# Order and due times of the transposing transfers of q and k in a chunked-attention and gated-FFN kernel

## The chip, the core and the metric

One core of one Trainium2 chip runs the whole program. The metric is the device time of one execution in microseconds (us), the median of several runs. The engines are named as in the profile: PE (TensorE, matmuls), PEld (its weight loads), DVE (VectorE), ACT (ScalarE), POOL (GpSimd, which here issues the loads from memory through the queue that the profile calls q0, software_dynamic) and SP (SyncE, which here issues the stores and the transposing transfers through q1, hardware_dynamic).

## What is computed

Attention over chunks of 32 rows, each with 8 memory keys, 16 rows of left and 8 rows of right context, then a gated feed-forward network over all 3072 rows (4 batches of 768), cut from the reference:

```python
for c in range(nc):                       # S // 32 = 24 chunks for each of 4 x 8 heads
    k_full = np.concatenate([mem_k, k[:, :, l_start:r_end]], axis=2)
    v_full = np.concatenate([mem_v, v[:, :, l_start:r_end]], axis=2)
    scores = scale * np.matmul(q_c, k_full.transpose(0, 1, 3, 2))
    scores = scores - np.max(scores, axis=-1, keepdims=True)
    a = np.exp(scores)
    a = a / (np.sum(a, axis=-1, keepdims=True) + 1e-09)
    out[:, :, c_start:c_end] = np.matmul(a, v_full)
...
gate = np.maximum(x @ w_gate, 0.0)        # x: 3072 x 512, w_gate and w_val: 512 x 1536
return ((gate * (x @ w_val)) @ w_out)     # w_out: 1536 x 512
```

## The kernel before

The 3072 rows are 24 tiles of 128 rows, numbered a = 0 to 23, six to a batch. Each tile goes through one chain of steps. q and k of the tile are loaded by POOL (`load_qk`, line 187). Both are transposed, so that the head's 64 elements lie on the partitions. `scores` (line 234) is 32 small matmuls on PE; row maximum, subtraction, row sum, reciprocal and normalisation are on DVE and the exponent on ACT. The probabilities p are transposed, `values` (line 305) multiplies them with v on PE, and `x_copy` brings the result to the block's x tile. The feed-forward network runs over seven blocks of 3, 3, 4, 4, 4, 4 and 2 tiles. A block is 12 pairs of groups of four matmuls, gate and value (`first`, line 325, the tiles g_ps and v_ps, from a ring of four PSUM buffers named fps), each pair with a relu on ACT and a product on DVE, and then, for each of its tiles, four groups of three matmuls that give out_ps (`second`, line 351). A copy on ACT to o_sb and a store by SP (`store`, line 359) end each tile. The attention of later tiles is woven between the matmuls of the network.

The transposition is done in two ways. For tiles below LATE_QK = 15, PE transposes q and k into PSUM (`qk_t`) and ACT or DVE copies them out (`qk_copy`). From tile 15 on, SP issues a transposing transfer from SBUF to SBUF (`qk_transfer`, line 214). That of q (called q15, q16 and so on below) lands in its place in qT. That of k (k15, k16, ...) lands in k_t, a ring of three buffers, and a key copy on ACT or DVE (`qk_copy`, lines 78 and 80 in the profile) spreads it into kT between the memory keys. The probabilities of tiles from LATE_P = 18 on are transposed by SP too (`p_transfer`, line 297). `scores` of tile a needs q of a and the key copies of a and, inside a batch, of a + 1; tile 17 is the last of its batch.

No engine chooses at run time. `schedule()` (line 568) simulates the kernel with costs written by hand and writes down one fixed instruction order for each engine; on the chip each engine goes through its order and waits on semaphores for what an instruction needs. An instruction that waits holds up all that stands behind it on its engine. The costs that touch the transposing transfers stand on one line:

```python
ISSUE, LAND, SLACK, LAND_P = 1.4, 12.0, 8.0, 3.0    # line 418
```

ISSUE is the time that SP is taken to be busy with one transfer. LAND is the time after which q may be used and the key copy may be planned. SLACK is how long after the planned landing of the load the transfer may be planned. LAND_P is the landing time of the transfer of p. These numbers only place instructions in the orders; the semaphores keep the result right whatever they are. The ring sizes (`room`, line 372) hold 3 k_t, 4 fps, 3 o_sb and 2 PSUM tiles for attention (aps).

Of the kernel before, what the change touches and what calls it, by code (L numbers as in the profile page):

```python
# [20 lines left out]
def kernel(  # L21
# [12 lines left out]
    nc = tc.nc  # L34
# [262 lines left out]
    def p_transfer(a):  # L297
        PT[a] = smpool.tile([128, HP, 128], F16, name="pT", bufs=6)
        nc.sync.dma_start(PT[a], P_n.pop(a).rearrange("p h a s -> p (h a s)"), transpose=True)
# [75 lines left out]
    def op(key, eng, fn, deps=(), prio=(0,), take=(), give=(), after=()):  # L375
        ops[key] = dict(eng=eng, fn=fn, deps=list(deps), prio=prio, take=list(take), give=list(give),
                        after=list(after))
# [4 lines left out]
    def psum(n):  # L382
        return {"ACT": 0.21 + 0.83e-3 * n, "DVE": 0.22 + 1.04e-3 * n}

    engine = {"ACT": nc.scalar, "DVE": nc.vector}
    MARGIN = 0.4


# [26 lines left out]
        return [("f", blk - 1, m, 0)] if m >= 0 else [("f", blk - 2, m + NDC, 0)]  # L415


    ISSUE, LAND, SLACK, LAND_P = 1.4, 12.0, 8.0, 3.0

    def pace_t(a):  # L420
        return [("s", a - 4)]
# [1 line left out]
    for a in range(NT):  # L423
        b, t = divmod(a, TPB)
        last = t == TPB - 1
        for i in (1, 0):
            if a >= LATE_QK:
                op(("t", a, i), {"SP": ISSUE}, lambda e, a=a, i=i: qk_transfer(a, i),
                   [(("qk", a, i), SLACK), ("new", b)],
                   (1, a - i, 0), ["kt"] if i else [], [("qk", LAND)], pace_t(a))  # L430
                if i:
                    op(("tc", a, i), {"DVE": 0.4, "ACT": 0.6}, lambda e, a=a, i=i: qk_copy(a, i, engine[e]),
                       [(("t", a, i), LAND)], (1, a - i, 0), (), ["kt"])
                continue
            op(("t", a, i), {"PE": 0.24}, lambda e, a=a, i=i: qk_t(a, i), [("qk", a, i), "ib", ("new", b)],
               (1, a - i, 0), ["aps"], ["qk"], pace(max(a - i, 0)))
            op(("tc", a, i), psum(HP * 128), lambda e, a=a, i=i: qk_copy(a, i, engine[e]), [("t", a, i)],
               (1, a - i, 0), (), ["aps"])
        op(("s", a), {"PE": 0.36}, lambda e, a=a: scores(a),
           [(("t", a, 0), LAND) if a >= LATE_QK else ("tc", a, 0), ("tc", a, 1)] + ([] if last else [("tc", a + 1, 1)]), (1, a, 1), ["sps"],  # L440
           ["kv"] if last else [], [("s", a - 1)] if a else [])
        op(("max", a), {"DVE": 0.74 + (0.2 if t == 0 or last else 0)}, lambda e, a=a: row_max(a), [("s", a)],
           (1, a, 2), ["mx"])
        op(("sub", a), {"DVE": 0.74}, lambda e, a=a: subtract(a), [("max", a)],
           (1, a, 3), ["dif"], ["sps", "mx"])
        op(("exp", a), {"ACT": 1.15}, lambda e, a=a: exponent(a), [("sub", a)], (1, a, 4), ["p"], ["dif"])
        op(("sum", a), {"DVE": 0.74}, lambda e, a=a: row_sum(a), [("exp", a)], (1, a, 5), ["sm"])
        op(("rec", a), {"DVE": 0.24}, lambda e, a=a: reciprocal(a), [("sum", a)], (1, a, 6), ["rinv"], ["sm"])
        op(("nrm", a), {"DVE": 0.74}, lambda e, a=a: normalise(a), [("rec", a)], (1, a, 7), ["pn"], ["p", "rinv"])
        if a < LATE_P:  # L450
            op(("p", a), {"PE": 0.24}, lambda e, a=a: p_t(a), [("nrm", a)], (1, a, 8), ["aps"], ["pn"])
            op(("pc", a), psum(HP * 128), lambda e, a=a: p_copy(a, engine[e]), [("p", a)], (1, a, 9), ["pT"], ["aps"])
        else:
            op(("pc", a), {"SP": ISSUE}, lambda e, a=a: p_transfer(a), [("nrm", a)], (0, a), ["pT"], [("pn", LAND_P)])
        blk = block_of[a]
        j = a - starts[blk]
        op(("v", a), {"PE": 0.45}, lambda e, a=a: values(a),
           [("pc", a) if a < LATE_P else (("pc", a), LAND_P)] + [("vl", b, 0 if b else t // 3, n) for n in range(2 if b else 2 * HP)]
           + ([("mr", b, n) for n in range(2 * HP)] if b else []), (1, a, 10), ["aps"] + (["xT"] if j == 0 else []), ["pT"],
           [("v", a - 1)] if a else [])  # L460
        op(("x", a), psum(HP * 128), lambda e, a=a: x_copy(a, engine[e]), [("v", a)], (1, a, 11), (), ["aps"],
           [("x", a - 1)] if a else [])
# [105 lines left out]
    def schedule():  # L568
# [20 lines left out]
        def ready(o, t, margin=0.0):  # L589
            if any(d not in started for d in o["after"]):  # L590
                return False
            for d in o["deps"]:
                d, lag = d if timed(d) else (d, 0.0)
                if d not in done or done[d] + lag + margin > t + 1e-9:
                    return False
            return all(room[r] >= o["take"].count(r) for r in o["take"])

        while len(started) < len(ops) + len(loads):
            t = heapq.heappop(times)
            while times and times[0] <= t + 1e-9:  # L600
                heapq.heappop(times)
            for g in [g for g in gives if g[0] <= t + 1e-9]:
                gives.remove(g)
                room[g[1]] += 1
            flying = [f for f in flying if f > t]
            moved = True
            while moved:
                moved = False
                for e in ("POOL", "PE", "ACT", "DVE", "SP"):
                    if free[e] > t + 1e-9:  # L610
                        continue
                    if e == "POOL":
                        if n_load == len(loads):
                            continue
                        o = loads[n_load]
                        if len(flying) >= 8 or not ready(o, t):
                            continue
                        n_load += 1
                        key = o["key"]
                        if o["n"]:  # L620
                            end = t + 0.62 + 0.27e-3 * o["n"]
                            queue_end = max(queue_end, end + 0.8) + o["work"]
                            flying.append(queue_end + 1.0)
                            done[key] = queue_end + (1.2 if n_load < 8 else 2.4 if n_load < 45 else 6.0 if key[0] == "vl" else 4.0)
                        else:
                            end = done[key] = t + max(o["work"], 0.6)
                        fn = o["fn"]
                    else:
                        o = None
                        for _, key in todo[e]:  # L630
                            late_pe = e == "PE" and t > 36.0 and ops[key]["prio"][0] == 1
                            if ready(ops[key], t, MARGIN if late_pe else 0.0):
                                o = ops[key]
                                break
                        if o is None:
                            continue
                        for x in o["eng"]:
                            todo[x].remove((o["prio"], key))
                        d = o["eng"][e] * (1.8 if e == "PE" and t < 24.0 and key[0] in ("t", "p") else 1.0)
                        end = t + d  # L640
                        done[key] = end + (0.25 if e == "PE" else 0.08)

                        if queue_end > t:
                            queue_end += 1.4 if e == "SP" and key[0] in ("t", "pc") else 0.7 if key[0] == "oc" else 0.0
                        fn = lambda o=o, e=e: o["fn"](e)
                        for g in o["give"]:
                            g, lag = g if isinstance(g, tuple) else (g, 0.0)
                            gives.append((done[key] + lag, g))
                            heapq.heappush(times, done[key] + lag)
                    for r in o["take"]:  # L650
                        room[r] -= 1
                    started.add(key)
                    for k in users.get(key, ()):
                        missing[k] -= 1
                        if not missing[k]:
                            offer(k)
                    order.append((t, fn))
                    free[e] = end
                    for x in (end, done[key], done[key] + 0.2, done[key] + 1.5, done[key] + MARGIN):
                        heapq.heappush(times, x)  # L660
                    moved = True
            assert times, [k for k in ops if k not in started][:20]
# [34 lines left out]
```

## Time and profile before

| what | us |
|---|---|
| median of 3 runs | 250.13 |
| the three runs | 254.63, 250.13, 247.74 |
| the profiled execution's own time | 251.15 |
| its span in the trace | 249.4 |
| PE busy in the span | 225.3 (90%) |
| DVE, ACT, POOL busy | 136.1, 108.3, 99.8 |
| mean granted TensorE clock | 0.993 |

What lies around the span is 251.15 - 249.4 = 1.75 us. PE's busy time is spread unevenly: the first 40 us hold 21.5 us of it (3.2, 3.5, 7.8 and 7.0 us in the four stretches of 10 us), and from 40 to 240 us every stretch of 10 us but one is full.

DMA work by queue, with the time that the packets took as a share of the span of 16 engines (packets of both queues overlap in an engine, so the shares can add up to more than the span):

```profile
q0 software_dynamic: 106912, 17.02, 94.6%
q1 hardware_dynamic: 18624, 9.72, 20.2%
```

The groups that belong to the transposing transfers and their key copies (line, engine, operation, count: shortest, median and longest duration in ns, first and last start in us). The duration is that of the issue on SP, not of the transfer:

```profile
L220 SPq DMA_TRANSPOSE k_t<-qk_b x9: 1206/1833/2962, 90.7 to 167.5; - x9
L220 SPq DMA_TRANSPOSE qT<-qk_b x9: 1194/1862/4265, 93.2 to 171.0; - x9
L80 DVE COPY kT<-k_t x5: 282/284/647, 116.2 to 180.7; 128x512 bf16<-128x512 bf16 x5
L78 ACT COPY kT<-k_t x4: 610/614/622, 112.1 to 166.4; 128x512 bf16<-128x512 bf16 x4
```

### The profile page before, as it was taken

What the parts mean: (1) busy time and instruction counts of PE and PEld (TensorE: products, weight loads), DVE (VectorE), ACT (ScalarE), POOL (GpSimd) and SP (SyncE); (2) the same over time, 40 slices, a digit from 0 to 9 for tenths busy, and PEclk for the clock granted to TensorE, in tenths of its full rate; (3) what the DMA queues carried; (4) which work ended last, traced back from release to release, by engine and by line L of the source; (5) the groups of instructions that cost most, each with busy time, mean ns of one, the idle gap of its engine ahead of it and who ended that gap; (6) DMA issues with size and microseconds to landing.
All of it is one profiled execution on the core that took longest, in us unless ns stands there. A gap on an engine that the chain in (4) does not pass through costs nothing.

```text
span 249.4 us, 5672 instructions
## 1 busy us (share of the span) xinstructions
PE 225.3 (90%) x2317; PEld 122.3 (49%) x2317; DVE 136.1 (55%) x252; ACT 108.3 (43%) x238; POOL 99.8 (40%) x118
## 2 busy tenths in 40 slices
PE   1546768999999999999999879999999999999995
PEld 0325445656644545555544434544544544444873
DVE  2986682477663257787066557678568043420430
ACT  3446553446434354554444352465443333321532
POOL 8999699994426773099920060000000000000000
PEclk9999999999999999999999988999999999999999
DMA  9999999999999999999999999333201410003102
GB/s 70 104 109 128 168 143 176 170 126 195 148 143 193 207 192 139 130 69 154 177 144 138 94 121 111 107 110 63 42 3 23 148 42 0 4 7 119 46 0 84
DMA packets 125562, 27.10 MB, mean 109 GB/s; under 512 B 116576, under 2 KB 122464, under 8 KB 125536
## 3 DMA queue, kind: packets, MB, share of 16 engines
q0 software_dynamic: 106912, 17.02, 94.6%
q1 hardware_dynamic: 18624, 9.72, 20.2%
q8 instruction: 18, 0.29, 0.5%
q14 instruction: 8, 0.07, 0.1%
HBM read 33.24 MB, written 6.29 MB: 159 GB/s over the span
## 4 chain that ended last, share of the span: by engine, by line
PE 75%; DMA 10%; POOL 9%; SPq 2%; issue 1%; ACT 1%; ACTq 0%; POOLq 0%
PE out_ps L356 25%; PE v_ps L331 22%; PE g_ps L331 21%; DMA w_val_sb<-in_moe_w_val_dram 5%; DMA k_t<-qk_b 5%; POOL qk_b L191 4%; POOL v_bd L169 3%; PE xT_ps L312 3%; SPq L220 2%; PE qk_ps L212 2%; PE s_ps L246 1%; POOL w_gate_sb L104 1%; PE pT_ps L295 1%; ACT g_relu L337 0%; POOL w_val_sb L104 0%
## 5 line engine op out<-in xcount | busy, mean ns | idle before, releaser
L343 DVE TENSOR_TENSOR gvT<-v_ps,g_relu 128x512 f16<-128x512 f32 (+2 forms) x84 | 51.5, 614 | 54.0 <-PE v_ps L331 39.6
L331 PE MATMUL v_ps<-xT,w_val_sb 128*128 128x512 f16 (+2 forms) x336 | 77.0, 352 | 1.9 <-DMA w_val_sb<-in_moe_w_val_dram 1.9
L331 PE MATMUL g_ps<-xT,w_gate_sb 128*128 128x512 f16 (+2 forms) x336 | 77.5, 354 | 0.4 <-DMA w_gate_sb<-in_moe_w_gate_dram 0.4
L337 ACT ACTIVATE g_relu<-g_ps 128x512 f16<-128x512 f32 (+2 forms) x84 | 44.9, 535 | 63.2 <-PE g_ps L331 53.1
L356 PE MATMUL out_ps<-w_out_sb,gvT 128*128 128x512 f16 (+2 forms) x300 | 65.6, 370 | 0.0
L331 PEld LDWEIGHTS <-w_gate_sb 128*128 128x128 f16 x336 | 32.2, 99 | 28.1 <-issue 2.0
L331 PEld LDWEIGHTS <-w_val_sb 128*128 128x128 f16 x336 | 31.6, 98 | 27.4 <-issue 2.1
L356 PEld LDWEIGHTS <-gvT 128*128 128x128 f16 x300 | 27.9, 98 | 29.7
L169 POOL DMA_DIRECT2D v_bd<-in_v_dram x24 | 28.0, 1201 | 7.9 <-issue 5.3
L78 ACT COPY o_sb<-out_ps 128x512 f32<-128x512 f32 (+2 forms) x25 | 14.2, 566 | 30.3 <-PE out_ps L356 30.2
L191 POOL DMA_DIRECT2D qk_b<-in_k_dram x24 | 23.2, 968 | 8.7 <-issue 5.2
L274 ACT ACTIVATE p_exp<-dif 128x256 f16<-128x256 f32 (+2 forms) x72 | 19.5, 337 | 12.5 <-DVE dif L266 12.5
L191 POOL DMA_DIRECT2D qk_b<-in_q_dram x24 | 22.8, 952 | 3.1 <-PE v_ps L331 2.8
L145 POOL DMA_DIRECT2D v_bd<-vmem x16 | 10.2, 676 | 28.9 <-DMA v_bd<-in_v_dram 28.9
L259 DVE TENSOR_REDUCE mx<-s_ps 128x8 f32<-128x512 f32 x24 | 16.5, 687 | 5.8 <-PE s_ps L246 5.5
L212 PE MATMUL qk_ps<-ident_b,qk_b 128*128 128x128 bf16 x120 | 13.8, 254 | 5.7 <-DMA qk_b<-in_q_dram 2.6
L278 DVE TENSOR_REDUCE sm<-p_exp 128x8 f32<-128x512 f16 x24 | 16.3, 679 | 2.9 <-ACT p_exp L274 2.8
L289 DVE TENSOR_TENSOR p_n<-p_exp,rinv 128x512 f16<-128x512 f16 x24 | 16.5, 687 | 0.4
L266 DVE TENSOR_TENSOR dif<-s_ps,mx 128x512 f32<-128x512 f32 x24 | 16.3, 678 | 0.2
L312 PEld LDWEIGHTS <-v_bd 128*128 128x128 f16 x384 | 12.7, 97 | 5.6 <-issue 1.9
L80 DVE CAST xT<-xT_ps 128x512 f16<-128x512 f32 x9 | 6.2, 692 | 16.9 <-PE xT_ps L312 16.9
L312 PE MATMUL xT_ps<-pT,v_bd 128*128 128x32 f16 x384 | 13.2, 178 | 1.9 <-ACT pT L78 1.8
(40 smaller groups left out, 112.1 us busy)
## 6 DMA issues: line engine op xcount, KB each, us to landing
out_dram<-o_sb SPq DMA_DIRECT2D x23, 256.0 KB
v_bd<-in_v_dram POOLq DMA_DIRECT2D x5, 672.0 KB, 16.7
qk_b<-in_k_dram POOLq DMA_DIRECT2D x24, 128.0 KB, 5.4
qk_b<-in_q_dram POOLq DMA_DIRECT2D x24, 128.0 KB, 4.8
w_gate_sb<-in_moe_w_gate_dram POOLq DMA_DIRECT2D x8, 192.0 KB, 5.0
w_val_sb<-in_moe_w_val_dram POOLq DMA_DIRECT2D x8, 192.0 KB, 6.2
w_out_sb<-in_moe_w_out_dram POOLq DMA_DIRECT2D x2, 768.0 KB, 11.1
v_bd<-in_v_dram POOLq DMA_DIRECT2D x15, 84.0 KB, 5.3
```

The lines of the kernel that those rows point to most:

```text
L169: nc.gpsimd.dma_start(dst[64 * par + s0:64 * par + s1, c0:c1, D * par:D * par + D], bass.AP(tensor=v.tensor, offset=v[b, HP * par, 0, 0].o ...
L191: nc.gpsimd.dma_start(qk_b[a, i], bass.AP(tensor=x.tensor, offset=x[b, 0, 128 * t, 0].offset, ap=[[D, 128], [S * D, H], [1, D]]))
L212: nc.tensor.transpose(ps[:, hp, :], x[:, 2 * hp:2 * hp + 2, :].rearrange("p h d -> p (h d)"), ident_b)
L259: nc.vector.reduce_max(SM[a, "mx"], s4, axis=AX.X)
L266: nc.vector.tensor_tensor(out=SM[a, "dif"].rearrange("p (m r) a s -> p r m a s", r=2), in0=S_ps.pop(a).rearrange("p r (m a) s -> p r m a s ...
L274: nc.scalar.activation(p[:, :, :, s0:s0 + k1 - k0], dif[:, :, :, k0:k1], ACT.Exp, scale=SCALE)
L289: nc.vector.tensor_tensor(out=P_n[a], in0=SM.pop((a, "p")), in1=rinv_b, op=ALU.mult)
L312: nc.tensor.matmul(ps[:, hp, r], lhsT=v_bd[b % NSET][:, hp, 4 * t + g, :], rhs=x[:, hp, r], start=True, stop=True)
L331: nc.tensor.matmul(ps, lhsT=w[:, f, 128 * m:128 * m + 128], rhs=xTs[blk][:, f, :], start=(f == 0), stop=(f == NFC - 1))
L337: nc.scalar.activation(st["r", m], st.pop((0, m)), ACT.Relu)
L343: nc.vector.tensor_tensor(out=st["gv"][:, m, :], in0=st.pop((1, m)), in1=st.pop(("r", m)), op=ALU.mult)
L356: nc.tensor.matmul(st["o", t, c], lhsT=st["gv"][:, m, 128 * t:128 * t + 128], rhs=w_out_sb[:, m, c[0]:c[1]], start=(m == 0), stop=(m == ND ...
```

## The change

The planner's numbers change, and nothing else: a transposing transfer of q or k counts as 1.8 us of SP instead of 1.4, may be planned 2 us behind its load instead of 8, and counts as landed after 14 us instead of 12; that of p counts as 1.3 us of SP instead of 1.4.

```diff
-    engine = {"ACT": nc.scalar, "DVE": nc.vector}
+    engine = {"ACT": nc.scalar, "DVE": nc.vector, "POOL": nc.gpsimd}
...
-    ISSUE, LAND, SLACK, LAND_P = 1.4, 12.0, 8.0, 3.0
+    ISSUE, LAND, SLACK, LAND_P = 1.8, 14.0, 2.0, 3.0
...
-            op(("pc", a), {"SP": ISSUE}, lambda e, a=a: p_transfer(a), [("nrm", a)], (0, a), ["pT"], [("pn", LAND_P)])
+            op(("pc", a), {"SP": 1.3}, lambda e, a=a: p_transfer(a), [("nrm", a)], (0, a), ["pT"], [("pn", LAND_P)])
...
-                    if e == "POOL":
+                    if e == "POOL" and not any(ready(ops[k], t) for _, k in todo[e]):
```

The first and the last hunk would let POOL take a planned operation, but no operation of the program names POOL as its engine (the key copies name DVE and ACT), so both are without effect, and POOL's order is the same in both kernels.

What the new numbers do to the orders, by comparing the two built programs:

- All orders are the same up to the middle of the fourth block or a little ahead of it; the number of instructions of each kind is the same.
- SP, from the first store of the third block (S1 to S4 are its four stores) to the last transfer before the stores of the fourth block. Before: S1, S2, S3, q16, S4, k17, q17, k18, q18, k19, q19, k20, q20, k21, q21, k22. After: S1, q16, S2, k17, q17, S3, S4, k18, q18, k19, q19, k20, q20, q21, k21, k22. Behind that the transfer p19 goes ahead of q22 and k23, and p23 stands one store earlier or later among the last.
- Key copies from k_t: 4 on ACT and 5 on DVE before; 8 on ACT and 1 on DVE after. Copies of p from PSUM: 16 on ACT and 2 on DVE before, 14 and 4 after. Copies of x: 15 and 9 before, 16 and 8 after.
- In the fourth block, the key copy of tile 17 stands on DVE ahead of the eighth product before, and on ACT behind the sixth relu after. `scores` of tile 16 stand on PE behind the ninth gate group before, and behind the seventh after. The key copy of tile 18 stands on ACT behind the ninth relu in both; after, the exponent of tile 16 stands ahead of it too.

## The prediction

> **What bounds the kernel now.** I read the page's slices first, to see where PE, the busiest engine, is not full.
>
> ```profile
> PE   1546768999999999999999879999999999999995
> PEclk9999999999999999999999988999999999999999
> DMA  9999999999999999999999999333201410003102
> ```
>
> Each digit is 6.2 us. PE is full from the eighth slice on, except for the 23rd and 24th (137 to 150 us, PE at 8 and 7) and the last, which ends with the final store; the clock falls only in the 24th and 25th (143 to 156 us). The first seven are the start, whose orders the change leaves alone. So what can be won lies around 140 to 155 us. PE's own waits from 60 us to the end are two, and ACT's and DVE's waits name the cause:
>
> ```profile
> PE xT_ps L312 <- ACT pT L78: 1.6, 1, 1.6
> PE s_ps L246 <- DVE kT L80: 0.8, 1, 0.8
> ```
>
> ```profile
> ACT kT L78 <- DMA k_t<-qk_b: 4.7, 1, 4.7
> DVE kT L80 <- DMA k_t<-qk_b: 2.5, 1, 2.5
> ```
>
> The chain of waits between 120 and 156 us says the same in order of time (start, length, what):
>
> ```profile
> 128.37 2.96 SPq L220
> ...
> 131.42 1.61 SPq L220
> ...
> 133.12 12.75 DMA k_t<-qk_b
> ...
> 146.42 0.59 ACT g_relu L337
> 147.01 0.48 ACT pT L78
> ...
> 147.54 0.55 PE xT_ps L312 x16
> 148.09 1.45 PE v_ps L331 x4
> 149.54 1.71 PE g_ps L331 x4
> 151.25 1.12 PE v_ps L331 x4
> ```
>
> k18 is issued at 133.12 and lands 12.75 us later. ACT stands at its key copy from 141.20 to 145.90, the relus behind it come late, fps fills up, and PE stops. Why k18 is issued only then, SP's timeline shows:
>
> ```profile
> 116.20 6.14 SPq L363 DMA_DIRECT2D out_dram<-o_sb  x3
> 122.43 4.26 SPq L220 DMA_TRANSPOSE qT<-qk_b  x1
> 126.79 1.49 SPq L363 DMA_DIRECT2D out_dram<-o_sb  x1
> 128.37 2.96 SPq L220 DMA_TRANSPOSE k_t<-qk_b  x1
> ```
>
> From 116.20 to 122.43 SP mostly waits for ACT's copies to o_sb (they begin at 115.59, 118.58 and 121.39, 0.58 each); from 122.43 to 151.3 it issues without a pause. The loads of q16 to k22 leave POOL between 107.05 and 116.65 and land within 3.6 to 5.3 us, so by 122 none holds up a transfer. It is SP's order, with stores ahead of transfers, that makes k17 and k18 late.
>
> **What the stall costs.** Two terms, from PE's busy time by stretches: from 139 to 148 us PE is busy 6.56 of 9.00 us, so 2.44 us idle. From 148 to 152.3 the granted clock is 0.60, and the three groups of four matmuls in the chain take 1.45 + 1.71 + 1.12 = 4.28 us where such a group takes 0.86 elsewhere: 4.28 - 3 x 0.86 = 1.70 us. Together 4.14 us. That is all there is to win here.
>
> **SP's new order.** No transfer is added; they move past stores. S1 is issued at 116.20 as before. A store's issue takes 1.49 us (the row above). A transfer's takes between the median of 1.86 us and the 4.26 and 2.96 us of q16 and k17 in this trace. With medians, and 0.1 us between issues: q16 at 117.8, S2 (ready at 119.2) at 119.8, k17 at 121.3, q17 at 123.2, S3 and S4 (ready at 122.0 and 125.0) at 125.2 and 126.8, k18 at 128.4. With the long issues (4.26, 2.96, 1.61): k17 at 123.7, k18 at 131.6. Before they were at 128.37 and 133.12. So k17 comes 4.7 to 7.1 us earlier and k18 1.5 to 4.7. The stores behind them cost nothing: S3 and S4 are issued at most 7 us later than before, and ACT next needs an o_sb buffer at 155.35.
>
> **When they land.** Transfers issued between 122 and 133 us land after 12.76 us (k17, released at 141.13), 12.75 (k18) and 14.2 (q17: PE's weight load waits for it until 145.66). Those of 90 to 96 us land, by the landing records of the trace, after 8.3 to 8.7 us, though the DMA engines are as full there (9 in every slice). The nearest are k17's and k18's own, so I take 12.75 and keep 8.6 and 14.2 as bounds. k17 lands at 134.1 to 136.5 (ends 129.9 and 137.9); k18 at 141.1 to 144.4 (ends 137.0 and 145.8).
>
> **When they are wanted.** The key copy of 17 now stands on ACT behind the sixth relu of the fourth block, which runs at 134.79 for 0.60 us: wanted at 135.4 (on DVE it was wanted at 141.13 - 2.53 = 138.6). `scores` 16 stand behind the seventh gate group, which ends at 136.5. The key copy of 18 stands behind the ninth relu, 140.60 for 0.60 us; two `scores` of 0.31 us are now ahead of that on PE: wanted at about 141.8, up to 0.8 us later if the exponent of 16 is in the way. So k17 is between 1.3 us early and 1.1 us late, and k18 between 0.7 us early and 2.6 us late. Behind a late copy stand, on ACT, the copy of p14 or the tenth relu; ACT has 1.07 us of idle time before each relu there, so PE loses what goes beyond that: nothing for k17 on ACT, 0.7 us where `scores` 16 wait for the copy (136.5 + 0.61 - 136.5, rounded up), 1.5 us for k18. The loss is 0 to 2.2 us. I take 0.5, because the walk with medians gives about none.
>
> **The other parts.** Four key copies go from DVE (0.28 us) to ACT (0.61), two copies of p from ACT (0.58) to DVE (0.42), one copy of x from DVE to ACT: ACT gets 1.9 us more in 60 us in which it is about half idle. Without that cover each copy would cost its 0.6 us once. k20, k21 and k22 wait for a k_t buffer, freed by the copies of 17, 18 and 19 at about 136, 143 and 147; their copies are wanted after 152, so 12.75 us fit. p19 now goes ahead of q22 and k23, when DMA is at 0 to 4: p18's transfer lands in 2.4 us there by the landing records. POOL's loads of v for the last batch share the engines with transfers that come earlier; the first user, `values` 18, is at 166.58, and POOL is through with waiting for them at 144.74, so 20 us cover it.
>
> **Sum.** 251.15 - 2.44 - 1.70 + 0.5 = 247.5 against the profiled execution. That execution is 1.02 above the median of its runs, and the median less the same 3.64 is 246.5. I forecast 247.0.
>
> **Rivals.**
> (1) *The lateness only moves.* k18 comes behind the same seven transfers of SP's queue in both orders, and q0 has as much to move. If the pause of q1 from 123.6 to 127 us, the one thing that earlier issues fill, is not worth more than it seems, k18 lands as late as before against a wish no later than before, and half or more of the stall is back: 249 to 251. For it: q0 is busy through it (111% of 16 engines between 117 and 150 us). Against it: k17 is two places further ahead. The Trainium skill says, in DMA: Bandwidth & Descriptors, under "Issuing engines are not separate DMA queues", that DMAs of all issuers interleave on the same 16 engines; that speaks for this rival, and the trace agrees in that both queues are slow together.
> (2) *The clock falls without the stall.* Between 30 and 40 us PE idles 3.0 us and the clock stays at 1.00; here 2.44 us idle precede 0.60. If the fall has another cause, 1.70 stays: 249.2. For my sum: it comes within 1 us of the stall's end, and nowhere else. The Trainium skill's rule (TensorE: Matmul & The Clock Gate, "Part 1: The HAM clock gate") is that the clock is gated after an idle window of about 3.4 us; the longest gap here is 1.6 us, so by it the fall would not come from this stall.
> (3) *Slower: the early transfers starve behind POOL's loads of v.* They now enter while q0 is fullest. q17 landed only at 145.6, just after POOL's loads were through at 144.74. If k17 must wait for that as well, ACT stands at its copy from 135.4 to 145.5, and PE, after 1 us, about 9 us, plus 1.70 of clock: 247.0 + 10.7 = 257.7. It decides from a landing of k17 after about 143, that is, a latency above 20 us. Against it: k17 landed at 141.1, before that end, and nothing in the trace took over 14.2.
> (4) *Nothing changes*: the orders do differ on SP, so only by (1).
>
> **Numbers.** Forecast 0.56 (245.3 to 248.5), (1) 0.22, (2) 0.07, (3) 0.08, and 0.07 for less than 245.3, if the start, which varies from run to run, comes out well. The range 245.0 to 250.8 leaves out (3), the far end of (1) and a little below. A comparison of this kernel tells about 2% from no change; 2% of 250.13 is 5.0, more than the 4.14 that the stall is worth. Faster by over 2% needs the last case, or the forecast against a repeat of before near its upper runs (252 or more; one of three was): 0.07 + 0.56 x 0.23 = 0.20. Slower is (3) and a tail: 0.09. The rest, 0.71, is within 2%.
>
> **What would show it.** Right: no wait of ACT or DVE for k_t above 1 us, k17 issued before 124 and k18 before 132, PE full from 130 to 160 and the clock at 9 there, `scores` 16 at about 136.5. Wrong: k17's copy released after 138, or PE losing time at a new place behind ACT.

## The result and the profile after

| | before | after |
|---|---|---|
| median of 16 runs each, us | 250.93 (247.74 to 254.63) | 247.05 (245.94 to 249.26) |
| profiled execution, us | 251.15 | 247.31 |
| span in the trace, us | 249.4 | 245.5 |
| mean granted TensorE clock | 0.993 | 1.000 |

The ratio of the times is 0.9887, 95% interval 0.9854 to 0.9919: faster by 1.1%, clear of noise but inside the 2% band. Such a ratio leaves out runs more than 1.5% above the fastest run of the same kernel, which here can be the runs with the longest stall, so medians of all runs stand beside it below (here 247.05 to 250.93, 1.5%). The spread of the runs shrinks too, from 6.9 to 3.3 us.

The page's slices after, the rows that the prediction showed of before:

```profile
PE   1545879999999999999999999999999999999994
PEclk9999999999999999999999999999999999999999
DMA  8999999999999999969999999973102310002102
```

The hole of PE in the 23rd and 24th slices and the dent of the clock behind it are gone; the start is as uneven as before. The list of waits after has no line for k_t, and PE's list from 60 us on is empty. Busy time by stretches (the columns are PE, PEld, DVE, ACT and POOL busy with the number of instructions, granted clock, DMA share, GB/s), first before:

```profile
139.00:148.00 9.00, 6.56 (x109) 3.24 (x107) 4.18 (x8) 3.23 (x8) 3.26 (x5) 1.00 1.36 115
148.00:152.30 4.30, 4.30 (x17) 1.59 (x14) 2.75 (x6) 2.11 (x7) 0.68 (x1) 0.60 1.83 96
```

and after:

```profile
139.00:148.00 9.00, 9.00 (x94) 4.51 (x93) 7.18 (x16) 5.43 (x12) 0.00 (x0) 1.00 1.82 109
...
148.00:152.30 4.30, 4.30 (x66) 2.27 (x65) 3.26 (x7) 1.30 (x5) 0.34 (x1) 1.00 1.51 74
```

PE is busy 9.00 of 9.00 us where it was busy 6.56, and the clock is 1.00 where it was 0.60. SP's timeline after:

```profile
117.37 0.34 SPq L363 DMA_DIRECT2D out_dram<-o_sb  x1
117.80 1.28 SPq L220 DMA_TRANSPOSE qT<-qk_b  x1
119.82 0.33 SPq L363 DMA_DIRECT2D out_dram<-o_sb  x1
120.24 2.12 SPq L220 DMA_TRANSPOSE k_t<-qk_b  x1
122.46 2.04 SPq L220 DMA_TRANSPOSE qT<-qk_b  x1
124.59 2.23 SPq L363 DMA_DIRECT2D out_dram<-o_sb  x2
126.93 2.87 SPq L220 DMA_TRANSPOSE k_t<-qk_b  x1
```

q16 goes out in the gap between the first two stores and takes SP 1.28 us, not 4.26; k17 is issued at 120.24 (128.37 before) and k18 at 126.93 (133.12 before). On the other queue POOL issues its three loads of v for the last batch at almost the same time in both kernels, first before, then after:

```profile
117.52 5.10 POOL L169 DMA_DIRECT2D v_bd<-in_v_dram  x3
```

```profile
117.90 5.12 POOL L169 DMA_DIRECT2D v_bd<-in_v_dram  x3
```

Before, q16 comes out at the end of these loads and k17 and k18 behind them. After, q16 comes out just ahead of them, k17 and q17 among them, and k18 behind them. The key copies on ACT find them there; none of these rows carries a wait:

```profile
135.92 0.61 ACT L78 COPY kT<-k_t 128x512 bf16<-128x512 bf16 x1
...
142.13 0.61 ACT L78 COPY kT<-k_t 128x512 bf16<-128x512 bf16 x1
...
146.55 0.63 ACT L78 COPY kT<-k_t 128x512 bf16<-128x512 bf16 x1
```

By the landing records k17 lands at 129.64, k18 at 137.79 and k19 at 141.68, so 6.3, 4.3 and 4.9 us ahead of these copies. The margin differs from one execution to another: in a second trace of the same kernel, taken for comparison with the experiments below, it is 6.1, 3.9 and only 0.5 us.

To keep the stall apart from the luck of the start, I read one stretch in every trace: from PE's first out_ps matmul of the third block to its first out_ps matmul of the fourth. Before it is 112.56 to 152.21, 39.65 us; after 113.19 to 148.61, 35.42. So the stretch holds 4.23 us of gain, while the part ahead of it came out 0.63 us later in this execution.

### The profile page after: what moved, and what is told of

It is laid out like the page before. It is cut to its first block, busy times and chain, and to the rows that moved or that the text cites. A ratio compares the mean times of both kernels' runs of the same rounds, so it can differ in the third digit from the quotient of the medians.

```text
span 245.5 us, 5666 instructions
## 1 busy us (share of the span) xinstructions
PE 225.5 (92%) x2317; PEld 122.1 (50%) x2317; DVE 137.3 (56%) x249; ACT 110.1 (45%) x241; POOL 100.1 (41%) x118
## 4 chain that ended last, share of the span: by engine, by line
PE 85%; POOL 8%; DMA 3%; DVE 1%; issue 1%; ACT 0%; DVEq 0%; POOLq 0%
PE v_ps L331 26%; PE out_ps L356 26%; PE g_ps L331 25%; POOL qk_b L191 5%; PE xT_ps L312 3%; DMA w_val_sb<-in_moe_w_val_dram 3%; POOL v_bd L169 3%; PE s_ps L246 2%; PE qk_ps L212 2%; PE pT_ps L295 1%; POOL w_gate_sb L104 1%; DVE gvT L343 0%; DVE p_n L289 0%; ACT pT L78 0%; DVE dif L266 0%
## 5 line engine op out<-in xcount | busy, mean ns | idle before, releaser
L212 PEld LDWEIGHTS <-qk_b 128*128 128x128 bf16 x120 | 9.3, 111 | 10.7 <-DMA qk_b<-in_k_dram 4.7
```

What stands on the lines that cost most here:

```text
L212: nc.tensor.transpose(ps[:, hp, :], x[:, 2 * hp:2 * hp + 2, :].rearrange("p h d -> p (h d)"), ident_b)
```

## The experiments

Two theories were set against each other: A, that SP's order alone is the cause (q16, k17 and q17 no longer stand behind the stores); and B, that it is the longer landing, with the key copies on ACT. Each run was timed against before on the same chip.

**E1: the order alone.** Three transfers of before get a new place in the program's order; every other engine keeps its own.

```diff
-        order, n_load = [], 0
+        order, n_load, at = [], 0, {("t", 16, 0): 117.5, ("t", 17, 1): 119.9, ("t", 17, 0): 120.0}
...
-                    order.append((t, fn))
+                    order.append((at.get(key, t), fn))
...
-        return order
+        return sorted(order, key=lambda x: x[0])
```

> Before, with three transfers moved in SP's order and nothing else: q16 ahead of the second store of the third block, k17 and q17 ahead of the third (as after has them). PE, ACT, DVE and POOL keep their orders. Theory A (the order of SP is the cause): k17 lands at about 130 and k18 at about 138, as in the trace of after; before wanted them at 138.6 (DVE) and 141.2 (ACT), so no wait of ACT or DVE for k_t, the clock stays at 1.00, and the time is that of after, 246.5 to 247.7 us. Rival B (the longer landing, 14 instead of 12 us, and the key copies on ACT are the cause): the waits stay at 2 to 5 us and the time at 250 to 251.

The instructions of PE, PEld, DVE, ACT and POOL stand in the trace in the same order as before. Measured: 247.62 us (median of 4) against 250.94, ratio 0.9881 (0.9803 to 0.9959). No wait for k_t in the trace. Here LAND is 12 and five of the nine key copies are on DVE as before, and the gain is whole. B falls.

**E2: the order undone.** After, with the same three transfers put back behind the stores (the two other lines that change are those of E1, here and in E7, E8 and E9):

```diff
+        order, n_load, at = [], 0, {("t", 16, 0): 123.4, ("t", 17, 1): 125.0, ("t", 17, 0): 126.2}
```

> After, with only q16, k17 and q17 moved back behind the stores in SP's order, as before has them; the key copies stay on ACT and all other orders stay. Theory A: k17 lands at about 141 as before, but stands on ACT where it is wanted at 135.9, so ACT waits about 5 us, PE loses about 4, and if the clock falls with the stall 0 to 2 us more: 251 to 253.5, slower than before. Rival B: no stall, 247. On the clock: if a stall brings its fall, the granted clock is under 1 within a few us of this one; if it has another cause, it stays at 1.00.

Measured: 254.41 (252.17 to 256.29, 4 runs) against 250.94, ratio 1.0126 (1.0009 to 1.0243). So it is slower than before, barely clear of noise. The stall is back and longer than in before: the copy of 17 now stands on ACT behind a relu that ends at 134.69, where DVE wanted it at 138.6 before (3.2 us earlier, when both are counted from the first out_ps matmul of the third block), and `scores` of tile 16, which need it, stand two gate groups earlier on PE. From the waits of E2, all and then PE's from 60 us on (line waited for: us in total, times, longest):

```profile
ACT kT L78 <- DMA k_t<-qk_b: 5.7, 2, 5.5
```

```profile
PE s_ps L246 <- ACT kT L78: 4.7, 1, 4.7
```

And the stretches of E2:

```profile
130.00:140.00 10.00, 6.15 (x37) 2.78 (x36) 4.39 (x8) 1.79 (x3) 0.63 (x1) 1.00 1.68 117
140.00:150.00 10.00, 9.13 (x109) 4.33 (x109) 6.20 (x12) 5.99 (x14) 3.93 (x5) 0.83 1.48 114
```

PE loses 3.85 us of the first and 0.87 of the second, one gap of 4.7 us, and at its end the clock falls, to 0.83 on the average of the second. The due times of after, without its order, make the kernel slower than before.

**E3: LAND = 14 alone** (ISSUE 1.4 and SLACK 8 as before).

```diff
+    ISSUE, LAND, SLACK, LAND_P = 1.4, 14.0, 8.0, 3.0
```

> Before with LAND = 14 alone (ISSUE 1.4, SLACK 8). SP keeps the order of before for q16 to k18; the key copies of 17 (ACT) and 18 (DVE) are placed 0.8 and 1.8 us later than before. Theory A: k17 comes 0 to 1 us late, k18 2 to 3 late but on DVE, so part of the stall stays: 248.3 to 250.3. Rival B: all of the gain, 247.

Measured: 250.83 (246.25 to 253.39, 10 runs) against 250.94: nothing gained in the median, where I had expected half. The ratio, 0.9890 (0.9799 to 0.9981), rests on the two shortest of the ten runs, 246.25 and 249.19, which have no trace. In the trace, of a run of 251.84, the transfers came even later than in before (k17 at 144.61, k18 at 148.18), and ACT waited 4.8 us and DVE 1.1.

**E4: SLACK = 2 alone** (ISSUE 1.4, LAND 12).

```diff
+    ISSUE, LAND, SLACK, LAND_P = 1.4, 12.0, 2.0, 3.0
```

> Before with SLACK = 2 alone (ISSUE 1.4, LAND 12). SP's order from q16 to k18 is that of after; the key copies of 17, 18, 19 and 20 are wanted 2 to 3 us earlier than in after, at about 133, 141, 145 and 150.5, against landings of 130, 138, 142 and 149 in the trace of after. Theory A: no wait for k_t above 1 us, 246.5 to 247.7. Rival B: the copies come too early with 12 us, a wait of some us and 249 to 251.

Measured: 247.00 (246.31 to 253.54, 5 runs) against 250.94, ratio 0.9852 (0.9741 to 0.9962). No wait for k_t, stretch 35.52 us. SLACK alone brings SP's new order from q16 to k18, and it is enough; ISSUE and the 1.3 us for p were not tried alone. The traced run, 249.63, is long through its start (see the end); the one of 253.54 has no trace.

**E5: before without POOL's loads of v for the last batch.** All orders stay as in before. That batch's values then use what the buffer held.

```diff
     def load_v_rows(b, par, s0, s1, c0, c1):
+        if b == B - 1: return
```

> Before, without POOL's three loads of v for the last batch (the last batch's values then use what the buffer held, so the output of that batch is not the reference's); all orders, SP's too, stay. Theory L (q1's transfers are slow because POOL has just filled the engines with those loads): q16 is issued in under 2 us instead of 4.3, and q16, k17, q17 and k18 land within 9 us instead of 11.6 to 14.2; then nothing waits for k_t and the time is 246.5 to 247.7. Rival (the transfers hold up one another, eight in a row in one queue): k17 and k18 still take 11 to 13 us and the time stays at 250 to 251.

Measured: 246.69 (246.48 to 247.90, 4 runs) against 252.45 on that chip, ratio 0.9831 (0.9758 to 0.9905). With the late order of before, SP's timeline of E5 now reads:

```profile
116.33 6.14 SPq L363 DMA_DIRECT2D out_dram<-o_sb  x3
122.56 1.79 SPq L220 DMA_TRANSPOSE qT<-qk_b  x1
125.17 0.33 SPq L363 DMA_DIRECT2D out_dram<-o_sb  x1
125.59 1.28 SPq L220 DMA_TRANSPOSE k_t<-qk_b  x1
```

q16 costs SP 1.79 us at the same time at which it cost 4.26. q16, k17, q17 and k18 land after 4.5, 6.0, 8.3 and 6.8 us, eight transfers in a row or not. So it is POOL's loads of v, issued between 117.5 and 122.6 in before, that make the transfers behind them as slow as they were there. What is left above the 2.4 us that k20, issued at 138.92, takes in this same trace can come from other loads or from the transfers one behind another; E5 doesn't separate these.

**E6: after with LAND = 8.**

```diff
+    ISSUE, LAND, SLACK, LAND_P = 1.8, 8.0, 2.0, 3.0
```

> After with LAND = 8 instead of 14: SP's order of q16 to k18 is that of after, the key copies of 17 to 20 are wanted at about 129.7, 137.3, 141.3 and 145. Against the landings in the trace of after (129.6, 137.8, 141.7, 148.7) k17 to k19 are up to 0.5 us late and k20 2 to 4: ACT waits 2 to 5 us in all and the time is 248.5 to 251. If the due times do not matter once the transfers are early, 247.

Measured: 248.56 (247.07 to 255.19, 4 runs), ratio to before 0.9876 (0.9780 to 0.9972); the same chip gave 247.08 for after. The trace has one wait of ACT for k_t, 0.8 us, and none of PE; its stretch is 35.19. The 2 to 5 us of waiting did not come in it: earlier copies also free the k_t buffers earlier, and k20 landed at 143.83, not at 148.7. The median is higher, but four runs with one at 255.19 don't settle by how much. That 14 us is needed is not shown; E4 does with 12.

**E7 and E9: tiles 13 and 14 transposed by SP too.** After, LATE_QK = 13, with the three transfers placed as in after.

```diff
-    LATE_QK, LATE_P = 15, 18
+    LATE_QK, LATE_P = 13, 18
...
+        order, n_load, at = [], 0, {("t", 16, 0): 117.0, ("t", 17, 1): 119.1, ("t", 17, 0): 119.2}
```

Four expectations follow, of E7, of after beside it, of E9 (the same kernel with more runs) and of after beside that:

> After with LATE_QK = 13: SP transposes q and k of tiles 13 and 14 too, and PE no longer does; q16, k17 and q17 are placed in SP's order as in after. PE is full from 40 us to the end in after, so it should be faster by what PE is spared, four groups of four transposes of 0.22 us: 0.9 us, 246.0 to 246.4. Rival: four more transfers between 88 and 96 us, behind POOL's loads of v for the third batch, come late, and a new wait for k_t at 104 to 112 takes it back: 247 to 249.

> After, unchanged, on the same chip as these three, to compare with: 246.5 to 247.6.

> The kernel with SP transposing tiles 13 and 14 too, again with more rounds: 0.3 to 0.9 us faster than after, 246.2 to 246.8.

> After, unchanged, with the same rounds on the same chip: 246.8 to 247.4.

Measured: the kernel takes 246.57 us against 247.08 for after (4 runs each) on one chip, and 246.90 against 246.97 (6 runs each) on another, each time a little above the range expected of it; ratios to before 0.9821 (0.9753 to 0.9888) and 0.9842 (0.9747 to 0.9936), then 0.9887 (0.9833 to 0.9941) and 0.9888 (0.9843 to 0.9932). In the traces, from the first out_ps matmul to the last it takes 171.23 and 171.24 us, against 172.11, 172.29 and 172.12 in the three traces of after: 0.9 us less, as worked out. The times can't tell it, because the first out_ps matmul comes anywhere between 68.8 and 72.4 us in the 13 profiles. It is the quickest of the kernels from there on that compute everything; that it beats after in time is not shown.

**E8: q16 alone moved.**

```diff
-        order, n_load = [], 0
+        order, n_load, at = [], 0, {("t", 16, 0): 117.5}
```

> Before with q16 alone moved ahead of the second store of the third block; k17, q17 and all the rest stay. Theory A with L: q16 enters before POOL's loads of v and no longer takes 4 to 5 us of SP behind them, so k17 is issued right behind the fourth store at about 126 instead of 128.4 and k18 at about 129.5 instead of 133; with 9 to 12 us to land they come at 135 to 138 and 139 to 141.5, wanted at 138.6 and 141.2: little or no wait, 246.8 to 248.5. If all three moves are needed, half of the stall or more stays: 249 to 251.

Measured: 252.12 (247.63 to 254.52, 13 runs) against 250.65, ratio 0.9955 (0.9904 to 1.0006). A miss, and the most telling one. The traced run is the longest of the 13, so what follows shows how the stall comes back, not how long it usually is; the shorter runs, down to 247.63, have no trace. q16 is quick (1.38 us of SP, landed 7.5 us after its issue), but now k17 is the first transfer behind POOL's loads, and takes their toll in its place. SP's timeline and the waits of E8:

```profile
116.76 1.38 SPq L220 DMA_TRANSPOSE qT<-qk_b  x1
119.32 6.18 SPq L363 DMA_DIRECT2D out_dram<-o_sb  x3
125.59 4.65 SPq L220 DMA_TRANSPOSE k_t<-qk_b  x1
```

```profile
ACT kT L78 <- DMA k_t<-qk_b: 7.2, 1, 7.2
```

All the profiled runs side by side (issue and landing in us from the start of the span; the landing is the last of the records of the transfer's semaphore; "wait" is of ACT and DVE for k_t):

| kernel | q16 issued, SP busy | k17 issued, landed | k18 issued, landed | wait | third to fourth block |
|---|---|---|---|---|---|
| before | 122.43, 4.26 | 128.37, 141.11 | 133.12, 145.88 | 7.2 | 39.65 |
| E3 LAND 14 | 122.68, 5.41 | 130.21, 144.61 | 134.15, 148.18 | 5.9 | 39.94 |
| E2 order undone | 121.72, 4.91 | 128.58, 140.18 | 133.03, 147.23 | 5.7 | 41.60 |
| E8 q16 moved | 116.76, 1.38 | 125.59, 139.48 | 132.36, 148.47 | 8.0 | 42.89 |
| E1 order alone | 117.50, 1.29 | 120.49, 128.93 | 126.33, 135.93 | 0 | 35.19 |
| after | 117.80, 1.28 | 120.24, 129.64 | 126.93, 137.79 | 0 | 35.42 |
| E4 SLACK 2 | 119.54, 1.26 | 122.53, 133.13 | 131.01, 141.37 | 0 | 35.52 |
| E6 LAND 8 | 117.02, 1.32 | 120.00, 128.95 | 125.85, 134.68 | 0.8 | 35.19 |
| E5 no v | 122.56, 1.79 | 125.59, 131.54 | 128.81, 135.59 | 0 | 35.19 |

What parts the traces with the stall from those without it, E5 apart, is the place of k17. In after, E1, E4 and E6 it is issued 0.9 to 2.3 us after POOL's first load of v begins. In before, E2, E3 and E8 no transfer is issued in the first 3.7 us of these loads.

## Why the prediction was right, and where it was off

- *Where the time lay.* Right. The two terms, 2.44 us of idle PE and 1.70 of low clock, make 4.14; the stretch gained 4.23, and from the first out_ps matmul of the third block to the last one of all it is 129.06 after and 133.51 before, 4.45. What the remaining 0.1 and 0.3 us are was not traced.
- *SP's order.* Right in kind, and a little too late: k17 was to be issued at 121.3 to 123.7 and was at 120.24, k18 at 128.4 to 131.6 and was at 126.93. Both came out ahead of the ranges, by 1.1 and 1.5 us, although the first store came 1.2 us later. A store had been taken at 1.49 us from S4 alone, which stands behind q16; S1 to S3 of the same trace take SP 0.33 to 0.34, and the four stores of after 0.33 to 1.16. q16 took 1.28 us where the median of 1.86 was put in.
- *When they land.* The mis-sized term. I took 12.75 us; k17 took 9.40 and k18 10.87. It landed just ahead of the near end that I kept (129.64 to 129.9), k18 inside. The nearest row was the wrong one to choose, since its 12.75 us were themselves made by the order that the change removes: with the order alone changed (E1) they are 8.44 and 9.60 us, and without POOL's loads of v in the old order (E5) 5.95 and 6.79. E8 shows that the place of q16 alone doesn't do it (13.89 and 16.11). Why k18, which is issued behind all of the loads in E1 and after too, is quicker there stays open. The quicker landing was not even needed: with 12.75 us from their new issues k17 and k18 would land at 133.0 and 139.7 (an estimate from these rows), still ahead of their copies at 135.92 and 142.13.
- *The loss of 0.5 us* did not come, since nothing was late. In the profiled execution the start came out 0.63 us later instead, so that the sum's 247.5 met 247.31 partly by luck. That the forecast of 247.0 met the median of 247.05 is luck in part too: it started from a median of 3 runs, 250.13, and the median of 16 is 250.93, so the gain between medians is 3.9 us where 3.1 was forecast.
- *What hides the rest.* The four key copies on ACT cost nothing: the copies stand in idle time and PE waits for nothing. POOL's loads of v came 7.2 us later in this trace (POOL waits for them until 151.96, not 144.74), but that is not a price of the early transfers: POOL waits until 145.16 and 150.18 in the two other traces of after, and until 145.35 in E1. I had given them 20 us of cover; in this trace the memory values that POOL loads behind them land at 155.9 and `values` 18 is at 163.61, so 7.7 are left.
- *Rival 1*, lateness that only moves: refuted for the copies that PE waits behind, k18 came 8.1 us earlier behind the same seven entries of its queue. It is true of later transfers, for which nothing waits: k20, q20 and q21 took 12.2, 15.3 and 13.5 us in this trace of after, 4.9, 6.0 and 6.6 in before. The pause of q1 that the rival builds on lasts from 123.1 to 125.9 us in the packet records, not from 123.6 to 127. The Trainium skill's sentence (DMA: Bandwidth & Descriptors, "Issuing engines are not separate DMA queues") agrees with E5, where the transfers of SP are quicker once POOL's loads are gone; it does not say that it matters which of two queues enters first, and E1, where three transfers enter earlier and nothing else changes, has the whole gain.
- *Rival 2*, a clock that falls for another cause: refuted here. In before, E2, E3 and E8 it falls in the last gap of PE or within 0.7 us behind it, to 0.50, for 3.41 us (6.83 in E8), and in no trace without a stall does it fall between 50 us and PE's last matmul. The rule of an idle window of about 3.4 us (the Trainium skill, TensorE: Matmul & The Clock Gate, "Part 1: The HAM clock gate") fits E2's gap of 4.7 us, but in before no gap was over 1.6 us and PE was busy 1.74 of the 3.41 us ahead of the fall, so there the trace does not agree with it. Nor is a half-idle stretch enough: from 33.75 to 37.16 us of before PE is busy 1.71 of 3.41 us and the clock stays at 1.00. What decides is open.
- *Rival 3*, starving behind the loads of v: it did not happen in after, where k17 and q17 go out among these loads and land after 9.4 and 9.3 us. Its mechanism is what E8's trace shows, with k17 and k18 taking 13.9 and 16.1 us, not 20, and the stretch 7.5 us longer than in after, where the rival had 10.7 over the forecast.

## What to carry to other kernels

A transfer's latency is not a constant to plan with: in this kernel the same 128 KB (q16 to k18) took 6 to 12 us where the first of them went out ahead of or among a burst of loads on the other queue, 12 to 16 where they came behind it, and 2.4 in the quiet. Before lengthening a planned landing, look at what stands in front of the transfer, on its issuing engine and on the other queue, and move it ahead. When a change has several numbers, find the one that alters an order: here SLACK alone did the work, and the later due times without the order cost time.

## What was not expected of the hardware

- *The issue itself slows down.* A transposing transfer takes SP 1.2 to 1.3 us in the quiet. Where none was issued in the first 3.7 us of POOL's loads of v, the next one took 4.26, 4.91, 5.41 and 4.65 us (before, E2, E3, E8), and 1.79 without those loads (E5). While SP issues q16 in before, no packet of q1 moves from 123.1 to 125.9 us. Being first behind the loads is not all of it: k18, which is that in after, took 2.87 us, and in E4 the third transfer, q17, took 4.40. Why was not tried.
- *The start varies.* The clock's records begin only at 28.4 to 36.2 us in the 13 traces (28.8 in before). Ahead of that the profile shows 1.00 without a record, and it can't have been full: in before gate and value matmuls start 320 ns apart there and 162 ns apart behind. So the mean of 0.993 counts most of the start as full. In E4's profile, where the records begin last, the clock fell once more, between 38 and 42 us, with no stall of the kind studied here:

```profile
38.00:42.00 4.00, 3.74 (x62) 2.76 (x63) 2.06 (x4) 2.25 (x5) 4.00 (x6) 0.70 1.26 181
```

There the first out_ps matmul comes at 72.42 us against 70.14 in after. With the stall gone, runs of after still differ by 3.3 us. In the three that have a trace (247.31, 247.43 and 246.37 us) the first out_ps matmul comes at 70.14, 70.07 and 69.19 us and the way from there to the last takes 172.1 to 172.3, so there it is the start, which the change doesn't touch; for the other runs that is not shown.
